# A routed feed-forward kernel: the second product's three terms added up in one PSUM bank

## The chip, the cores and the metric

The kernel runs on one core of a Trainium2 chip. The metric is the device time of one execution in microseconds; lower is better. A core has a matrix engine (TensorE; PE in the profile, its weight loads PEld), a vector engine (VectorE, DVE), a scalar engine (ScalarE, ACT), GpSimd (POOL) and a queue that issues transfers (SyncE, SP). TensorE writes into PSUM, an accumulator memory of eight banks of 512 float32 values per partition; VectorE and ScalarE read it out ("evict" it) into SBUF.

## What is computed

The reference does two things in float32. First a causal convolution of 7 taps along the sequence, with taps that are a softmax over the head's weights. Then a routed feed-forward network: each row picks one of 8 experts, goes through that expert's two matrices with a ReLU between them, and is scaled by the softmax probability of its expert.

```python
B, S, D = 8, 3584, 192; E, F = 8, 1024; N = B * S       # N = 28672 rows
out = np.einsum('hk,bskhg->bshg', w, x_unf)             # w: softmax of weight over 7 taps
...
logits = x @ w_gate + modality_bias[modality_id]
e_idx = np.argmax(logits, axis=1)
gate_w = probs[np.arange(N), e_idx]
for e in range(E):
    mask = e_idx == e
    h = np.maximum(x[mask] @ w1[e], 0.0)
    out[mask] = gate_w[mask, None] * (h @ w2[e])
```

## The kernel before, in words

The convolved rows are computed in groups (lines 222 to 392: products with a band matrix, then the gate's logits, the choice of expert, each row's place), and POOL scatters them to a buffer in DRAM, `routed_rows`, sorted by expert. Beside each row stand its gate and its place in the output. A slot is 512 such rows (256 in the last chunk) of one expert; a pass is 256 rows. `Slot` (from line 602 on) brings a slot's weights and rows, splits the weights, and turns the rows with TensorE transposes.

All large products are done in a format (F32R) in which TensorE takes one pass. To keep accuracy, each factor is split into a high and a low part: `split` casts the high part on ScalarE (L99) and subtracts on VectorE for the low part (L100). A product of two split factors is then three products: high by high, high by low and low by high.

The first product (`first`, L686) makes 256 hidden values for 256 rows: ten products of 256 columns into a bank `hps`, of which ScalarE makes `hh`, the high part of the ReLU (L689), and VectorE `hl`, the low part (L690). The second product (`second`) takes `hh` and `hl` as the stationary operand, 128 hidden values by 128 rows, and streams the second matrix past them. In SBUF that matrix lies as `w2b`: for each block c of 128 hidden values, 192 columns of the high part followed by 192 of the low part. For each block (two in a step) and each half j of the rows, there is one product of `hh` with all 384 columns (L704), which puts high by high into the accumulator's columns 0 to 191 and high by low into 192 to 383, and one of `hl` with the 192 high columns (L708), added to columns 0 to 191. A pass is four steps, eight blocks. Each half has an accumulator `po` of its own, in a bank of its own; there are two such banks (`ps_g2`), so a pass takes both.

After a pass, `put` evicts: for each half ScalarE multiplies the columns 192 to 383 by the gate into `lowp` (L720), VectorE multiplies the columns 0 to 191 by the gate and adds `lowp` (L722) into `o`, one of five buffers, and POOL scatters `o` to the output's rows (L723).

`run` (L810) sets the order: in each step the first product of the step, then the second product of the step two before (LAG = 2), then pieces of the routing work of later rows, as many as are due, splits of the next slot's weights, and at one step of each pass the transposes of the next pass. ScalarE keeps the order in which the program is written (`ORDERED`, L878); the order of the other engines is set by a scheduler.

Of the kernel before, what the change touches and what calls it, by code (L numbers as in the profile page):

```python
# [9 lines left out]
F32 = mybir.dt.float32  # L10
# [3 lines left out]
AF = mybir.ActivationFunctionType  # L14
ALU = mybir.AluOpType
# [3 lines left out]
P = 128  # L19
# [24 lines left out]
def conv_then_routed_ffn(ctx, tc, x, weight, modality, w_gate, mod_bias, w1, w2, out):  # L44
    nc = tc.nc
    NB, S, D = x.shape
    H, K = weight.shape
    E, _, FF = w1.shape
# [6 lines left out]
    NF = FF // P  # L55
    NJ = T // P
# [17 lines left out]
    sp = ctx.enter_context(tc.tile_pool(name="sp", bufs=4))  # L74
    hp = ctx.enter_context(tc.tile_pool(name="hp", bufs=4))
    ps_g1 = ctx.enter_context(tc.tile_pool(name="ps_g1", bufs=2, space=PSUM))
    ps_g2 = ctx.enter_context(tc.tile_pool(name="ps_g2", bufs=2, space=PSUM))
# [5 lines left out]
    def ring(pool, n, shape, dtype, name, tag=None):  # L83

        tag = tag or name
        k = turns[tag] = turns.get(tag, -1) + 1
        return pool.tile(shape, dtype, name=name, tag=f"{tag}_{k % n}", bufs=1)
# [22 lines left out]
    def warm(n):  # L110
# [9 lines left out]
        out=tri, in_=ones, compare_op=ALU.is_gt, fill=0.0, base=0,  # L120
# [481 lines left out]
    class Slot:  # L602
# [90 lines left out]
        def second(self, k, fp):  # L693
            wb = w2b[self.i % 2]
            hh, hl = self.h.pop((k, fp))
            if fp == 0:
                self.po = [ring(ps_g2, 2, [P, 2 * D], F32, "po") for _ in range(NJ)]
            for u in range(2):
                c = 2 * fp + u
                for j, po in enumerate(self.po):  # L700
                    js = slice(j * P, (j + 1) * P)

                    def by_hi():
                        nc.tensor.matmul(po, hh[:, u, js], wb[:, c, :], start=c == 0, stop=c == NF - 1,  # L704
                                         skip_group_check=True)

                    def by_lo():
                        nc.tensor.matmul(po[:, 0:D], hl[:, u, js], wb[:, c, 0:D], start=False, stop=False,  # L708
                                         skip_group_check=True)

                    for product in (by_lo, by_hi) if c == NF - 1 else (by_hi, by_lo):
                        product()
            if fp == NF // 2 - 1:
                self.put(self.h.pop(("tag", k)))

        def put(self, tag):
            for j, po in enumerate(self.po):
                gate = tag[:, j, 0:1]
                lowp = ring(sp, 2, [P, D], F32, "lowp")
                nc.scalar.activation(out=lowp, in_=po[:, D:2 * D], func=AF.Copy, scale=gate)  # L720
                o = ring(sp, OUTS, [P, D], F32, "o")
                nc.vector.scalar_tensor_tensor(out=o, in0=po[:, 0:D], scalar=gate, in1=lowp, op0=ALU.mult, op1=ALU.add)  # L722
                st = nc.gpsimd.indirect_dma_start(  # L723
                    out=out, out_offset=bass.IndirectOffsetOnAxis(ap=tag.bitcast(I32)[:, j, 1:2], axis=0),
                    in_=o, in_offset=None, bounds_check=N - 1, oob_is_err=False).ins
                tc.declare_no_dep(st, group="out", reason="each row is written once")
                tc.add_to_no_dep_group("out", st)
# [3 lines left out]
    for chunk, groups in enumerate(GROUPS_OF_CHUNK):  # L731
# [3 lines left out]
        if chunk == len(GROUPS_OF_CHUNK) - 1:  # L735
            n = (tokens + E * (size - 1)) // size
        else:
            n = SLOTS_OF_CHUNK[chunk]
# [171 lines left out]
```

## Time and profile before

| what | value |
|---|---|
| runs shown | 1309.37 and 1307.13 us, median 1308.25 |
| profiled execution | 1306.6 us |
| its span, first to last instruction | 1304.9 us |
| mean granted TensorE clock | 0.983 |
| POOL busy | 525.4 us (40%) |
| DMA | 140.41 MB, mean 108 GB/s |
| chain that ended last | TensorE 80%, VectorE 6%, POOL 3% |

The profile is of one execution. A row of a group reads: line, engine, operation, tile written <- tiles read, shape and type, count | busy us, mean ns of one | idle time of the engine just before, and what released it. A row of the table by stretch has, for each engine, its busy us and its count of instructions. A row of the timeline has the start and the length in us. Products overlap on TensorE, and the ends of their records are modelled.

### The profile page before, as it was taken

The numbers are of one execution on the slowest core, as the hardware profiler recorded it, in microseconds if no ns is written. First come the engines' busy times: TensorE is split into PE (matmuls) and PEld (weight loads), VectorE is DVE, ScalarE is ACT, GpSimd is POOL, SyncE is SP. The second block draws the span as 40 slices with busy tenths as digits, with TensorE's granted clock in tenths as the row PEclk, the third lists the DMA queues.
The fourth block names the chain that finished last, engine by engine and source line by source line (L and its number), as shares of the span: only waits on it lengthen the run. The fifth ranks groups of instructions, "written<-read, shape, count | busy, mean of one in ns | idle before, by whom it ended". The sixth has DMA issues, their size and how long they took to land.

```text
span 1304.9 us, 27875 instructions
## 1 busy us (share of the span) xinstructions
PE 1253.3 (96%) x9448; PEld 1222.3 (94%) x9448; DVE 1074.7 (82%) x2576; ACT 785.0 (60%) x1828; POOL 525.4 (40%) x574
## 2 busy tenths in 40 slices
PE   8549999999999999999999999999999999999997
PEld 7338899999999999999999999999999999999996
DVE  6459978798889888898889988898888878777895
ACT  2126566566666566766666566666665556555674
POOL 4636753442626244362624435262532612112121
PEclk9859999999999999999999999999999999999999
DMA  5467432352326241453215432352223525353440
GB/s 164 148 172 208 130 117 59 92 151 81 86 65 166 80 116 51 122 157 94 75 45 161 114 96 76 92 158 83 60 61 91 146 67 109 80 156 114 129 117 18
DMA packets 155356, 140.41 MB, mean 108 GB/s; under 512 B 43714, under 2 KB 141627, under 8 KB 155204
## 3 DMA queue, kind: packets, MB, share of 16 engines
q1 hardware_dynamic: 130164, 93.58, 27.3%
q0 software_dynamic: 23232, 44.30, 10.7%
q8 instruction: 76, 1.25, 0.4%
q10 hardware_dynamic: 1808, 0.66, 0.2%
q14 instruction: 76, 0.62, 0.2%
HBM read 160.37 MB, written 48.25 MB: 160 GB/s over the span
## 4 chain that ended last, share of the span: by engine, by line
PE 80%; issue 7%; DVE 6%; POOL 3%; DMA 2%; ACT 1%; POOLq 0%; DVEq 0%; ACTq 0%
PE hps L686 35%; PE po L704 23%; PE po L708 11%; PE cv L274 5%; PE gt L318 3%; POOL routed_rows L211 2%; PE tp L660 1%; DMA routed_rows<-y,idx 1%; POOL out_dram L723 1%; DVE hl L690 1%; PE hps L114 1%; PE tp L661 1%; DMA out_dram<-o,tag 1%; DVE turned L298 1%; DVE gx L100 1%
## 5 line engine op out<-in xcount | busy, mean ns | idle before, releaser
L704 PE MATMUL po<-w2b,hh 128*128 128x384 f32 x1824 | 555.5, 355 | 2.1 <-DVE o L722 1.7
L686 PE MATMUL hps<-sxh,w1b 128*128 128x256 f32 x1824 | 491.7, 292 | 0.5 <-ACT sxh L668 0.4
L689 ACT ACTIVATE hh<-hps 128x512 fp32r<-128x512 f32 x456 | 273.6, 600 | 349.0 <-PE hps L686 342.6
L723 POOL DMA_INDIRECT out_dram<-o,tag x228 | 237.2, 1040 | 530.4 <-DVE o L722 464.6
L708 PE MATMUL po<-w2b,hl 128*128 128x192 f32 x1824 | 440.6, 252 | 0.0
L690 DVE SCALAR_TENSOR_TENSOR hl<-hps,hh 128x512 fp32r<-128x512 f32 x456 | 312.8, 686 | 108.7 <-ACT hh L689 103.6
L686 PE MATMUL hps<-sxs,w1b 128*128 128x256 f32 x1824 | 362.7, 280 | 0.2 <-DVE sxs L670 0.2
L704 PEld LDWEIGHTS po<-w2b,hh 128*128 128x128 f32 x1824 | 343.6, 188 | 5.5 <-DVE o L722 4.8
L686 PEld LDWEIGHTS hps<-sxh,w1b 128*128 128x128 f32 x1824 | 345.0, 189 | 3.7 <-ACT sxh L668 0.6
L708 PEld LDWEIGHTS po<-w2b,hl 128*128 128x128 f32 x1824 | 345.2, 190 | 0.0
L211 POOL DMA_INDIRECT routed_rows<-y,idx x256 | 255.0, 996 | 143.8 <-issue 72.1
L686 PEld LDWEIGHTS hps<-sxs,w1b 128*128 128x128 f32 x1824 | 280.2, 189 | 0.4 <-issue 0.4
L686 PE MATMUL hps<-sxl,w1b 128*128 128x256 f32 x912 | 256.5, 281 | 3.1 <-DVE sxl L670 3.1
L100 DVE TENSOR_TENSOR w1b<-raw,w1b 128x512 fp32r<-128x512 f32 x244 | 164.9, 682 | 19.6 <-ACT w1b L99 17.3
L686 PEld LDWEIGHTS hps<-sxl,w1b 128*128 128x128 f32 x912 | 173.6, 190 | 5.6 <-DVE sxl L670 3.3
L99 ACT CAST w1b<-raw 128x512 fp32r<-128x512 f32 x244 | 149.0, 619 | 0.0
L100 DVE TENSOR_TENSOR w2b<-raw,w2b 128x384 fp32r<-128x384 f32 x244 | 133.0, 551 | 10.2 <-ACT w2b L99 10.0
L99 ACT CAST w2b<-raw 128x384 fp32r<-128x384 f32 x244 | 122.7, 511 | 0.0
L279 ACT COPY y<-cv 112x192 f32<-112x192 f32 (+1 forms) x198 | 53.7, 318 | 96.2 <-PE cv L274 72.3
L720 ACT ACTIVATE lowp<-po,tag 128x192 f32<-128x192 f32 x228 | 83.6, 418 | 31.2 <-PE po L704 31.2
L722 DVE SCALAR_TENSOR_TENSOR o<-po,tag,lowp 128x192 f32<-128x192 f32 x228 | 84.8, 411 | 5.4 <-ACT lowp L720 2.3
L274 PE MATMUL cv<-x,band 128*112 128x384 f32 (+2 forms) x160 | 47.7, 427 | 22.1 <-ACT y L279 19.6
(135 smaller groups left out, 1107.4 us busy)
## 6 DMA issues: line engine op xcount, KB each, us to landing
raw<-in_moe_w_dram SPq DMA_DIRECT2D x61, 768.0 KB
raw<-in_moe_w_dram SPq DMA_DIRECT2D x61, 512.0 KB
raw<-in_moe_w_dram SPq DMA_DIRECT2D x122, 256.0 KB
xr<-in_x_dram SPq DMA_DIRECT2D x36, 384.0 KB
rows<-routed_rows SPq DMA_DIRECT2D x53, 260.0 KB
x<-in_x_dram SPq DMA_DIRECT2D x26, 384.0 KB
ends<-routed_rows SPq DMA_DIRECT2D x53, 128.0 KB
routed_rows<-y,idx POOLq DMA_INDIRECT x256, 2.9
```

The lines of the kernel that those rows point to most:

```text
L99: nc.scalar.copy(out=hi, in_=raw)
L100: return nc.vector.tensor_tensor(out=lo, in0=raw, in1=f(hi), op=ALU.subtract).ins
L211: routed(chunk, nc.gpsimd.indirect_dma_start(out=scr, out_offset=bass.IndirectOffsetOnAxis(ap=idx, axis=0), in_=src, in_offset=None,).ins)
L274: nc.tensor.matmul(cv, wt[:, h, :], xt[:, :, hs], start=n == 0, stop=n == len(terms) - 1)
L686: nc.tensor.matmul(hps[:, u, :], wa[:, c, fs], mv[z], start=n == 0, stop=n == len(terms) - 1)
L689: nc.scalar.activation(out=hh, in_=hps, func=AF.Relu)
L690: nc.vector.scalar_tensor_tensor(out=hl, in0=hps, scalar=0.0, in1=f(hh), op0=ALU.max, op1=ALU.subtract)
L704: nc.tensor.matmul(po, hh[:, u, js], wb[:, c, :], start=c == 0, stop=c == NF - 1, skip_group_check=True)
L708: nc.tensor.matmul(po[:, 0:D], hl[:, u, js], wb[:, c, 0:D], start=False, stop=False, skip_group_check=True)
L720: nc.scalar.activation(out=lowp, in_=po[:, D:2 * D], func=AF.Copy, scale=gate)
L722: nc.vector.scalar_tensor_tensor(out=o, in0=po[:, 0:D], scalar=gate, in1=lowp, op0=ALU.mult, op1=ALU.add)
L723: st = nc.gpsimd.indirect_dma_start(out=out, out_offset=bass.IndirectOffsetOnAxis(ap=tag.bitcast(I32)[:, j, 1:2], axis=0), in_=o, in_offse ...
```

## The change

The accumulator of a pass becomes one tile of 2 x 192 columns in one bank: half j has columns 192 j to 192 j + 191, and all three terms are added up there. The product of `hh` with 384 columns is split into one with the 192 high columns and one with the 192 low columns of `w2b`. In the last block the order of the three terms is reversed. Only the first product into the bank carries the start flag. Two banks are used in turn, one a pass. The eviction is one ScalarE instruction for each half, which multiplies by the gate and writes `o`; `lowp` and VectorE's part are gone.

```diff
@@ second @@
             if fp == 0:
-                self.po = [ring(ps_g2, 2, [P, 2 * D], F32, "po") for _ in range(NJ)]
+                self.po = ring(ps_g2, 2, [P, NJ, D], F32, "po")
             for u in range(2):
                 c = 2 * fp + u
-                for j, po in enumerate(self.po):
+                for j in range(NJ):
                     js = slice(j * P, (j + 1) * P)
-
-                    def by_hi():
-                        nc.tensor.matmul(po, hh[:, u, js], wb[:, c, :], start=c == 0, stop=c == NF - 1,
+                    terms = (hh, 0), (hh, 1), (hl, 0)
+                    if c == NF - 1:
+                        terms = terms[::-1]
+                    for n, (z, w) in enumerate(terms):
+                        nc.tensor.matmul(self.po[:, j, :], z[:, u, js], wb[:, c, w * D:(w + 1) * D],
+                                         start=c == j == n == 0, stop=c == NF - 1 and n == len(terms) - 1,
                                          skip_group_check=True)
-
-                    def by_lo():
-                        nc.tensor.matmul(po[:, 0:D], hl[:, u, js], wb[:, c, 0:D], start=False, stop=False,
-                                         skip_group_check=True)
-
-                    for product in (by_lo, by_hi) if c == NF - 1 else (by_hi, by_lo):
-                        product()
@@ put @@
-            for j, po in enumerate(self.po):
-                gate = tag[:, j, 0:1]
-                lowp = ring(sp, 2, [P, D], F32, "lowp")
-                nc.scalar.activation(out=lowp, in_=po[:, D:2 * D], func=AF.Copy, scale=gate)
+            for j in range(NJ):
                 o = ring(sp, OUTS, [P, D], F32, "o")
-                nc.vector.scalar_tensor_tensor(out=o, in0=po[:, 0:D], scalar=gate, in1=lowp, op0=ALU.mult, op1=ALU.add)
+                nc.scalar.activation(out=o, in_=self.po[:, j, :], func=AF.Copy, scale=tag[:, j, 0:1])
```

On TensorE, in one step in the middle of the program, the order was this from the end of the first product on (output <- streamed operand, stationary operand; the weight loads of these products are part of them and have no row):

```order
L686 MATMUL hps<-sxs,w1b_89 128x256 x2
L704 MATMUL po<-w2b_91,hh 128x384
L708 MATMUL po<-w2b_91,hl 128x192
L704 MATMUL po<-w2b_91,hh 128x384
L708 MATMUL po<-w2b_91,hl 128x192
L704 MATMUL po<-w2b_91,hh 128x384
L708 MATMUL po<-w2b_91,hl 128x192
L704 MATMUL po<-w2b_91,hh 128x384
L708 MATMUL po<-w2b_91,hl 128x192
L274 MATMUL cv<-xh,band_hi 112x384
```

At the same place it now is:

```order
L686 MATMUL hps<-sxs,w1b_89 128x256 x2
L706 MATMUL po<-w2b_91,hh 128x192 x2
L706 MATMUL po<-w2b_91,hl 128x192
L706 MATMUL po<-w2b_91,hh 128x192 x2
L706 MATMUL po<-w2b_91,hl 128x192
L706 MATMUL po<-w2b_91,hh 128x192 x2
L706 MATMUL po<-w2b_91,hl 128x192
L706 MATMUL po<-w2b_91,hh 128x192 x2
L706 MATMUL po<-w2b_91,hl 128x192
L274 MATMUL cv<-xh,band_hi 112x384
```

Eight products became twelve, and what stands before and after them on TensorE is the same.

On ScalarE, at the end of a pass, the order before, with what each instruction waits for (PE for TensorE's products, DMAHW for loads, DMASW for POOL's scatters):

```order
L689 ACTIVATE hh<-hps 128x512 [waits DVE_49,PE_49]
L720 ACTIVATE lowp<-po,tag 128x192 [waits PE_49] x2
L99 CAST xh<-xr 128x768 [waits DMAHW1_49]
L99 CAST w2b_760<-raw_1_88 128x2x192
L668 CAST sxh<-tp 128x256 [waits PE_49]
```

and at such a place now:

```order
L689 ACTIVATE hh<-hps 128x512 [waits DVE_49,PE_49]
L715 ACTIVATE o<-po,tag 128x192 [waits DMASW3_49,PE_49]
L715 ACTIVATE o<-po,tag 128x192 [waits DMASW4_49]
L99 CAST w2b_760<-raw_1_88 128x2x192
L668 CAST sxh<-tp 128x256 [waits PE_49]
```

The two evictions stand where they stood, and each now waits for a scatter too, the one that read its `o` buffer last.

## The prediction

> **What bounds the kernel now.** I read the page's busy shares first, then the table of engines by stretch, then the groups by line and shape, and last the timeline of TensorE's weight loads over one step.
>
> ```profile
> span 1304.9 us, 27875 instructions
> PE 1253.3 (96%) x9448; PEld 1222.3 (94%) x9448; DVE 1074.7 (82%) x2576; ACT 785.0 (60%) x1828; POOL 525.4 (40%) x574
> ```
>
> ```profile
> core 0: us, PE busy (x) PEld busy (x) DVE busy (x) ACT busy (x) POOL busy (x), PEclk, DMA share, GB/s
> 0.00:100.00 100.00, 64.31 (x329) 48.84 (x330) 56.68 (x235) 26.60 (x81) 48.90 (x77) 0.81 0.56 165
> 100.00:200.00 100.00, 95.45 (x685) 88.58 (x684) 88.48 (x220) 60.06 (x143) 66.65 (x69) 1.00 0.49 144
> 200.00:400.00 200.00, 199.73 (x1528) 196.34 (x1527) 172.78 (x405) 127.63 (x295) 78.00 (x83) 1.00 0.34 92
> 400.00:800.00 400.00, 399.12 (x3068) 395.82 (x3066) 351.52 (x810) 259.19 (x599) 177.94 (x192) 1.00 0.38 105
> 800.00:1200.00 400.00, 399.53 (x3110) 397.92 (x3109) 326.23 (x751) 245.06 (x563) 131.99 (x133) 1.00 0.37 99
> 1200.00:1295.00 95.00, 95.00 (x741) 94.79 (x740) 78.30 (x159) 65.83 (x150) 19.96 (x20) 1.00 0.35 100
> ```
>
> The columns that matter are PE and PEld, TensorE's products and its weight loads. From 200 us to 1295 us PE is idle for 0.27 + 0.88 + 0.47 + 0 = 1.6 us of 1095, at a granted clock of 1.00. Nothing else can set the time there: VectorE's 82% and ScalarE's 60% lie beside a TensorE that never waits. So each nanosecond added to TensorE's sequence goes onto the end one for one, and work taken off VectorE buys nothing. But PE busy is made of overlapping products (a record lasts until its result is out), so the price of a product is the distance between starts, not its recorded length. The groups show why that matters:
>
> ```profile
> L704 PE MATMUL po<-w2b,hh 128*128 128x384 f32 x1824 | 555.5, 355 | 2.1 <-DVE o L722 1.7
> L708 PE MATMUL po<-w2b,hl 128*128 128x192 f32 x1824 | 440.6, 252 | 0.0
> L704 PEld LDWEIGHTS po<-w2b,hh 128*128 128x128 f32 x1824 | 343.6, 188 | 5.5 <-DVE o L722 4.8
> L708 PEld LDWEIGHTS po<-w2b,hl 128*128 128x128 f32 x1824 | 345.2, 190 | 0.0
> ```
>
> The second product is 1824 pairs: one product of 384 columns, one of 192, each with a weight load of its own. Four pairs make a step, so there are 1824 / 4 = 456 steps. If recorded lengths were prices, a pair would take 355 + 252 = 607 ns, and 1824 of them 1107 us, 85% of the span with the first product still to be placed. They overlap, so the starts are what to read. Here is one step of the second product, TensorE's loads and three of its products (start, length):
>
> ```profile
> 1231.93 0.19 PEld L708 LDWEIGHTS po<-w2b,hl 128*128 128x128 f32 x1
> 1232.11 0.19 PEld L704 LDWEIGHTS po<-w2b,hh 128*128 128x128 f32 x1
> 1232.21 0.19 PEld L708 LDWEIGHTS po<-w2b,hl 128*128 128x128 f32 x1
> 1232.39 0.19 PEld L704 LDWEIGHTS po<-w2b,hh 128*128 128x128 f32 x1
> 1232.50 0.19 PEld L708 LDWEIGHTS po<-w2b,hl 128*128 128x128 f32 x1
> 1232.68 0.19 PEld L704 LDWEIGHTS po<-w2b,hh 128*128 128x128 f32 x1
> 1232.79 0.19 PEld L708 LDWEIGHTS po<-w2b,hl 128*128 128x128 f32 x1
> 1232.96 0.19 PEld L686 LDWEIGHTS hps<-sxh,w1b 128*128 128x128 f32 x1
> 1233.07 0.19 PEld L686 LDWEIGHTS hps<-sxl,w1b 128*128 128x128 f32 x1
> ```
>
> ```profile
> 1231.93 0.34 PE L704 MATMUL po<-w2b,hh 128*128 128x384 f32 x1
> 1232.10 0.25 PE L708 MATMUL po<-w2b,hl 128*128 128x192 f32 x1
> 1232.19 0.36 PE L704 MATMUL po<-w2b,hh 128*128 128x384 f32 x1
> ```
>
> The load for the next product starts when the present product starts to stream, and runs beside it. From 1231.93 to 1233.07 is 1.14 us for four pairs, 0.285 a pair. The distances alternate. After a load for hl (that is, while the 384 columns stream) they are 0.18, 0.18, 0.18, 0.17, mean 0.178. After a load for hh, or the last one for w1b (while the 192 columns stream), they are 0.10, 0.11, 0.11, 0.11, mean 0.108. The first 384-column product passes on after 0.17, so 192 columns are worth 0.085 to 0.09 of streaming, and the product rows say the same (1232.10 to 1232.19). The next load nevertheless starts only after 0.108: what is late is the load, not the columns. **A load of 128 columns cannot follow the one before it by less than about 0.108 us**; 384 columns hide that, 192 do not. The transposes, of only 128 columns, show the same floor:
>
> ```profile
> 1230.52 0.14 PEld L661 LDWEIGHTS tp<-ident,ends 128*128 128x128 f32 x1
> 1230.63 0.19 PEld L686 LDWEIGHTS hps<-sxh,w1b 128*128 128x128 f32 x1
> 1230.74 0.19 PEld L686 LDWEIGHTS hps<-sxl,w1b 128*128 128x128 f32 x1
> ```
>
> That is 0.11 twice. The mean of the six distances is (0.43 + 0.22) / 6 = 0.1083 us, the floor that I use.
>
> **The change part by part.** *Products.* Each pair (384, 192) becomes three products of 192: the same 576 columns, but three loads where there were two, 1824 more products and loads in all. Now a pair costs 0.285: one product bound by its columns, one by its load. In the change all three are bound by the load: 3 x 0.1083 = 0.325. A step goes from 1.14 to 12 x 0.1083 = 1.30 us, and 456 steps times 0.16 are **+73 us**. The step's two ends stay as they are, since the last product of a step is one of 192 before and after. Bounds from the rows: from below, if every product were bound by its columns alone (0.0875), a step would be 1.05 us, -0.09 x 456 = -41 us. From above, the distance that the first product's loads keep, beside 256 columns:
>
> ```profile
> 1233.07 0.19 PEld L686 LDWEIGHTS hps<-sxl,w1b 128*128 128x128 f32 x1
> 1233.19 0.19 PEld L686 LDWEIGHTS hps<-sxh,w1b 128*128 128x128 f32 x1
> ```
>
> 0.12, or 12 x 0.12 = 1.44 us a step, +0.30 x 456 = +137 us. I take 0.1083, since the rows it comes from stand in this very sequence, beside the same 192 columns.
>
> *The same weights twice.* In each triple hh is loaded for w2's high part and at once again for its low part. Does the second load count? The program has such neighbours already: the gate multiplies each block of wg_parts with gx's high and low part in turn.
>
> ```profile
> L318 PE MATMUL gt<-gx,wg_parts 128*128 128x256 f32 x336 | 49.9, 298 | 11.8 <-ACT gx L99 8.0 <-DVE gx L100 3.6
> L318 PEld LDWEIGHTS gt<-gx,wg_parts 128*128 128x128 f32 x336 | 44.7, 198 | 14.7 <-ACT gx L99 9.5 <-DVE gx L100 4.6 <-DVE y L281 0.3
> L114 PE MATMUL hps<-ones 112*112 112x448 bf16 x50 | 12.3, 404 | 1.2 <-DVE ones L109 1.2
> L114 PEld LDWEIGHTS <-ones 112*112 112x112 bf16 x50 | 7.4, 149 | 5.7 <-issue 1.7 <-DVE ones L109 1.2
> ```
>
> 336 products, 336 loads, though every second load brings what is there; the warm-up loads the same ones 50 times for 50 products. So the repeated load is issued, and I count it in full.
>
> *Evictions.* VectorE loses 228 instructions of 411 ns; ScalarE keeps 228 of the same shape, which now write o.
>
> ```profile
> L722 DVE SCALAR_TENSOR_TENSOR o<-po,tag,lowp 128x192 f32<-128x192 f32 x228 | 84.8, 411 | 5.4 <-ACT lowp L720 2.3 <-DMA out_dram<-o,tag 2.1 <-ACT w2b L99 1.0
> L720 ACT ACTIVATE lowp<-po,tag 128x192 f32<-128x192 f32 x228 | 83.6, 418 | 31.2 <-PE po L704 31.2
> L689 ACT ACTIVATE hh<-hps 128x512 fp32r<-128x512 f32 x456 | 273.6, 600 | 349.0 <-PE hps L686 342.6 <-issue 1.2
> ```
>
> The 84.8 us lie beside TensorE and are worth 0, but for the last eviction after the last product, some 0.4 us. ScalarE takes over the wait for a free o, which the output's scatter on POOL's queue must have read: 2.1 us in all on VectorE now. Behind it on ScalarE stand the casts of the next weights and hh, for which TensorE waits. But ScalarE itself idles 343 us waiting for TensorE ahead of hh, and the second product runs two steps after the first (LAG), about 2 x 2.33 us by the starts of the loads (1230.74 for one step's second load, 1233.07 for the next), so 2.1 us spread over the program cost 0. Without that cover they would cost those 2.1 us.
>
> *The banks.* Each pass's two accumulators shared two banks, so the next pass waited for the eviction: PEld 4.8 us and PE 1.7 us behind o, partly the same waits. With both halves in one bank and two banks in turn, that wait goes: I take **-4 us**, between 0 and -6.5. Nothing is late in its place: a bank is written again a whole pass after its eviction could begin.
>
> **Sum.** The profiled execution took 1306.6 us with its span of 1304.9. 1306.6 + 73 - 4 - 0.4 = 1375 us. The median of the runs shown, 1308.25, lies 1.65 above that execution, so about 1377; the rows are read to 0.01 us and a floor of 0.109 would add 4, so I say **1378 us**, 5.3% above now.
>
> **Rivals.** *Columns alone* (the other side): the load queue runs ahead far enough that 192-column products follow each other at 0.0875. Its place is all 456 steps, its price -41 - 4, the time 1263 us. It decides from a load distance below 0.095 (a third of 0.285); the rows above, 0.10 to 0.11 four times out of four beside just such products, speak against it. The Trainium skill, "TensorE: Matmul & The Clock Gate", section "Back-to-back issue gap", has a rule of this kind: a sustained stream of loads and products takes about 81 ns a product at 128 columns and 131 ns at 512. A line between these gives an estimate of 89 ns at 192, 12 x 0.089 = 1.07 us a step, about -32 us and 1272. The trace here disagrees (0.11 where only 128 columns stream), and the same page's section "LDWEIGHTS (loading the stationary operand)", columns / 1.2 or 107 ns, agrees with it.
>
> *The repeated load is free.* Then hh streams 2 x 0.0875, hl's load hides behind that, and the triple costs 0.175 + 0.108 = 0.283: the pair's price. 1308 - 4 = 1304 us, no change. The 336 loads for 336 products speak against it; the trace can't show whether such a load is shorter, because 256 columns cover it.
>
> *Loads at the wider distance*, 0.12 instead of 0.1083, because they now follow without a break: +137 - 4, 1441 us. Against it: the transposes' loads follow each other at 0.11 with no long stream among them.
>
> *ScalarE becomes the bound* through its new wait: every one of 114 evictions would have to outlast two steps before TensorE noticed. Its share is 60%, and the wait is 2.1 us in all; between 0 and +2 us, inside the range.
>
> **How the numbers follow.** A measurement of this kernel can tell about 2% from no change, 26 us. My forecast has 0.86: all triples bound by the load, 1362 to 1396 (a floor of 0.1055 to 0.112 us in the same sum: 12 x 0.1055 = 1.27 and 12 x 0.112 = 1.34 us a step). The wider distance and other additions beyond 1396 get 0.08, all slower. The free repeated load gets 0.04 (same), columns alone 0.02 (faster). So faster 0.02, same 0.04, slower 0.94. The range 1362 to 1396 leaves out 0.14.
>
> **What would show it.** In the changed profile: L706 with 5472 products and 5472 loads; loads of the second product 0.108 apart without alternation; a step of that product 1.30 us long; PE still idle for next to nothing after 200 us; VectorE at some 990 us busy and no PE wait for an eviction. Loads 0.09 apart, or two loads for three products, would make the forecast wrong; so would PE idle time of tens of microseconds behind ScalarE.

## The result and the profile after

The changed kernel takes 1391.21 us (median of 1390.91 and 1391.51) where the kernel before takes 1308.25: a ratio of 1.0633, 95% interval 1.0615 to 1.0650. It is 83 us slower; 1378 were forecast, with 1362 to 1396 as the range. The profiled execution took 1390.9 us. Its page begins:

```profile
span 1389.2 us, 31268 instructions
PE 1337.7 (96%) x11272; PEld 1312.5 (94%) x11272; DVE 997.3 (72%) x2348; ACT 780.9 (56%) x1828; POOL 524.2 (38%) x574
```

TensorE has 11272 - 9448 = 1824 more products and as many more loads; VectorE has 228 instructions fewer and 77 us less to do. The table by stretch of the changed kernel (the same columns as in the prediction) shows which of the two counts:

```profile
200.00:400.00 200.00, 200.00 (x1716) 197.59 (x1716) 150.87 (x336) 117.23 (x271) 76.43 (x84) 1.00 0.29 81
400.00:800.00 400.00, 399.85 (x3447) 399.20 (x3446) 309.78 (x710) 242.15 (x561) 158.50 (x170) 1.00 0.36 100
800.00:1200.00 400.00, 400.00 (x3476) 399.55 (x3475) 285.81 (x655) 232.99 (x540) 139.97 (x144) 1.00 0.32 86
1200.00:1380.00 180.00, 180.00 (x1585) 180.00 (x1583) 117.22 (x228) 106.95 (x244) 36.33 (x34) 1.00 0.37 106
```

After 200 us TensorE is idle for 0.15 us in all, at a granted clock of 1.00: it is still the only bound, and it has more to do. The groups of the second product and its eviction, changed kernel:

```profile
L706 PE MATMUL po<-w2b,hh 128*128 128x192 f32 x3648 | 630.4, 272 | 0.0
L706 PEld LDWEIGHTS po<-w2b,hh 128*128 128x128 f32 x3648 | 555.7, 191 | 0.0
L706 PE MATMUL po<-w2b,hl 128*128 128x192 f32 x1824 | 481.2, 274 | 0.0
L706 PEld LDWEIGHTS po<-w2b,hl 128*128 128x128 f32 x1824 | 341.3, 192 | 0.0
L715 ACT ACTIVATE o<-po,tag 128x192 f32<-128x192 f32 x228 | 83.6, 417 | 88.1 <-PE po L706 84.9 <-DMA out_dram<-o,tag 3.1
```

There are 5472 products and 5472 loads, so the second load of hh is there each time. The idle column is 0.0 where the kernel before had 1.7 and 4.8 us behind an eviction. And this is one step of the second product, the weight loads in order of time (x2 joins two neighbours; the second of a row of 0.30 starts 0.30 - 0.19 = 0.11 after the first):

```profile
1280.58 0.31 PEld L706 LDWEIGHTS po<-w2b,hh 128*128 128x128 f32 x2
1280.81 0.19 PEld L706 LDWEIGHTS po<-w2b,hl 128*128 128x128 f32 x1
1280.92 0.30 PEld L706 LDWEIGHTS po<-w2b,hh 128*128 128x128 f32 x2
1281.14 0.19 PEld L706 LDWEIGHTS po<-w2b,hl 128*128 128x128 f32 x1
1281.26 0.30 PEld L706 LDWEIGHTS po<-w2b,hh 128*128 128x128 f32 x2
1281.48 0.19 PEld L706 LDWEIGHTS po<-w2b,hl 128*128 128x128 f32 x1
1281.59 0.30 PEld L706 LDWEIGHTS po<-w2b,hh 128*128 128x128 f32 x2
1281.81 0.19 PEld L706 LDWEIGHTS po<-w2b,hl 128*128 128x128 f32 x1
1281.92 0.19 PEld L686 LDWEIGHTS hps<-sxh,w1b 128*128 128x128 f32 x1
```

The alternation of 0.18 and 0.11 is gone. Twelve loads take 1281.92 - 1280.58 = 1.34 us, 0.112 each, against 1.14 us for eight. 456 steps times 0.20 are 91 us. Read over all steps after 200 us, the median from a step's first load to the first load behind the step is 1.148 us before and 1.343 now, and 456 times 0.195 are 89 us. The span grew by 84.3. The waits for evictions that are gone make up for part of the products (before, 1.7 us on TensorE and 4.8 on its loads, partly the same). Against them stands a stretch of lower clock: behind two waits of TensorE for the gate's rows, 1.27 and 1.37 us, the granted clock is 0.50 from 160 to 165 us and products stand 0.21 us apart, where the kernel before has 1.00; I estimate some 3 us from these rows. So the balance closes to a few microseconds, not better.

### The profile page after: what moved, and what is told of

It reads as the page before. It is cut to its first block, busy times and chain, and to the rows that moved or that the text cites. A ratio compares the mean times of both kernels' runs of the same rounds, so it can differ in the third digit from the quotient of the medians.

```text
span 1389.2 us, 31268 instructions
## 1 busy us (share of the span) xinstructions
PE 1337.7 (96%) x11272; PEld 1312.5 (94%) x11272; DVE 997.3 (72%) x2348; ACT 780.9 (56%) x1828; POOL 524.2 (38%) x574
## 4 chain that ended last, share of the span: by engine, by line
PE 66%; issue 1%; POOL 0%; DMA 0%; ACT 0%; DVE 0%; POOLq 0%; ACTq 0%
PE po L706 32%; PE hps L686 29%; PE cv L274 2%; PE gt L318 2%; PE tp L660 1%; PE tp L661 1%; DMA out_dram<-o,tag 0%; POOL out_dram L716 0%; POOL routed_rows L211 0%; ACT hh L689 0%; ACT gx L99 0%; ACT w2b L99 0%; DVE hl L690 0%; PE rp L367 0%; PE rp L368 0%
## 5 line engine op out<-in xcount | busy, mean ns | idle before, releaser
L706 PE MATMUL po<-w2b,hh 128*128 128x192 f32 x3648 | 630.4, 272 | 0.0
L706 PEld LDWEIGHTS po<-w2b,hh 128*128 128x128 f32 x3648 | 555.7, 191 | 0.0
L686 PE MATMUL hps<-sxh,w1b 128*128 128x256 f32 x1824 | 491.5, 292 | 0.5 <-ACT sxh L668 0.4
L706 PE MATMUL po<-w2b,hl 128*128 128x192 f32 x1824 | 481.2, 274 | 0.0
L686 PE MATMUL hps<-sxs,w1b 128*128 128x256 f32 x1824 | 363.2, 281 | 0.3 <-DVE sxs L670 0.3
L686 PEld LDWEIGHTS hps<-sxh,w1b 128*128 128x128 f32 x1824 | 346.2, 190 | 3.6 <-ACT sxh L668 0.6
L706 PEld LDWEIGHTS po<-w2b,hl 128*128 128x128 f32 x1824 | 341.3, 192 | 0.0
L686 PEld LDWEIGHTS hps<-sxs,w1b 128*128 128x128 f32 x1824 | 280.5, 190 | 0.4 <-issue 0.4
L686 PE MATMUL hps<-sxl,w1b 128*128 128x256 f32 x912 | 256.7, 281 | 3.3 <-DVE sxl L670 3.3
L686 PEld LDWEIGHTS hps<-sxl,w1b 128*128 128x128 f32 x912 | 174.0, 191 | 5.7 <-DVE sxl L670 3.5
L715 ACT ACTIVATE o<-po,tag 128x192 f32<-128x192 f32 x228 | 83.6, 417 | 88.1 <-PE po L706 84.9
L100 DVE TENSOR_TENSOR gx<-turned,gx 128x768 fp32r<-128x768 f32 x56 | 53.5, 955 | 23.8 <-ACT gx L99 23.3
```

What stands on the lines that cost most here:

```text
L100: return nc.vector.tensor_tensor(out=lo, in0=raw, in1=f(hi), op=ALU.subtract).ins
L686: nc.tensor.matmul(hps[:, u, :], wa[:, c, fs], mv[z], start=n == 0, stop=n == len(terms) - 1)
L706: nc.tensor.matmul(self.po[:, j, :], z[:, u, js], wb[:, c, w * D:(w + 1) * D], start=c == j == n == 0, stop=c == NF - 1 and n == len(terms ...
L715: nc.scalar.activation(out=o, in_=self.po[:, j, :], func=AF.Copy, scale=tag[:, j, 0:1])
```

## The experiments

**Theory:** a load of 128 weight columns can follow the one before it only after 0.11 us, so a product costs the longer of that and its own streaming (0.0875 us for 192 columns). **Rivals:** the columns set the distance; each load and product has a fixed cost of issue; a repeated load of the same weights is special; part of the loss comes from the single bank or from ScalarE's eviction.

The first four runs fell on a chip where every kernel ran 200 to 250 us longer, before too (1542.7 us there). In the trace of the eviction alone from that chip, ScalarE stands idle ahead of `hh` for 177.7 us in 19 waits whose releaser the profile doesn't show, and TensorE for 35 to 49 us ahead of the products of each of L686, L704 and L708 with nothing shown to wait for. That the engines waited for their instructions, as the expectations say, fits this but is not shown. These times are given but not built upon; the same kernels were run again on other chips.

### The products alone

```diff
 def by_hi():
-    nc.tensor.matmul(po, hh[:, u, js], wb[:, c, :], start=c == 0, ...)
+    for w in range(2):
+        nc.tensor.matmul(po[:, w * D:(w + 1) * D], hh[:, u, js], wb[:, c, w * D:(w + 1) * D], start=c == w == 0, ...)
```

> The three products of 192 columns, but with the two banks of a pass and both evictions as before. Theory (the load sets each product's distance): the whole loss is here. The changed profile shows loads 0.111 to 0.112 us apart, a step of 1.34 us against 1.14, so 1308 + 456 x 0.20 = 1399 us, up to 8 less where waits of before go into the longer step: 1391 to 1400. Rival (part of the loss comes from the single bank or from the eviction on the scalar engine): clearly under 1391, by that part.

Measured there: 1601.9 us, a ratio of 1.0376 (1.0346 to 1.0407), which decides nothing, since TensorE's products alone do not set the time there.

> The kernel of products_alone once more, because there all kernels, before too, ran some 230 us longer, with ScalarE and TensorE waiting now and then for their instructions. Where they don't: theory, as there, before + 83 to 92 us (1391 to 1400 where before takes 1308), TensorE idle below 1% after 200 us. Rival (the single bank or the eviction cost part of the loss): clearly under before + 83.

Measured: 1397.95 us, 1.0680 (1.0658 to 1.0702), +89 us. The whole loss is in the products, as the theory has it. The changed kernel's 1.0633 lies 0.0047 below, 6 us: bank and eviction do not cost, they give. The groups of this run still have the wait for VectorE's eviction, and more of it than the kernel before (1.7 and 4.8 us there), so a few of the 89 us are this wait and not the loads:

```profile
L705 PE MATMUL po<-w2b,hh 128*128 128x192 f32 x3648 | 632.0, 272 | 5.6 <-DVE o L723 5.6
L705 PEld LDWEIGHTS po<-w2b,hh 128*128 128x128 f32 x3648 | 555.5, 191 | 7.7 <-DVE o L723 7.1
```

### The eviction alone

```diff
-lowp = ring(sp, 2, [P, D], F32, "lowp")
-nc.scalar.activation(out=lowp, in_=po[:, D:2 * D], func=AF.Copy, scale=gate)
-nc.vector.scalar_tensor_tensor(out=o, in0=po[:, 0:D], scalar=gate, in1=lowp, op0=ALU.mult, op1=ALU.add)
+nc.scalar.activation(out=o, in_=po[:, 0:D], func=AF.Copy, scale=gate)
```

> The products of before, 384 and 192 columns in two banks; the eviction is the scalar engine's alone and reads columns 0 to 191. The high by low term is computed and left out of the output. Theory: nothing hangs on the vector engine's part, 1302 to 1309 us. Rival (the scalar engine's new wait for a free output buffer delays hh): over 1312 us.

Measured: 1524.7 us, 0.988 (0.9855 to 0.9905) of before's 1542.7; again with those idle stretches.

> The kernel of evict_alone once more, where engines do not wait for instructions. The high by low term is computed and left out of the output. The changed kernel took 6 to 7 us less than the products alone, so bank and eviction together gave that. Theory (the bank gave it, the eviction nothing): 1306 to 1310 us where before takes 1308. Rival (the eviction without the vector engine gave it): 1300 to 1304.

Measured: 1303.5 us, 0.9957 (0.9941 to 0.9973), 5 us less. Here my expectation fell: the rival had 1300 to 1304. The group of the loads for hh in this run says how:

```profile
L704 PEld LDWEIGHTS po<-w2b,hh 128*128 128x128 f32 x1824 | 343.9, 189 | 0.7 <-ACT o L720 0.6
```

4.8 us of waiting for an eviction became 0.6, though the banks are as before. An eviction of one ScalarE instruction frees the bank sooner than one that goes on to VectorE; whether the second instruction or VectorE's queue made the difference is not kept apart here. So the spare bank and the shorter eviction remove the same wait, and either alone is enough for most of it.

### Fewer columns, the same loads

```diff
-nc.tensor.matmul(self.po[:, j, :], z[:, u, js], wb[:, c, w * D:(w + 1) * D], ...)
+wide = D if c == n == 0 else 128
+nc.tensor.matmul(self.po[:, j, 0:wide], z[:, u, js], wb[:, c, w * D:w * D + wide], ...)
```

> As the changed kernel, but the products of the second stage stream 128 columns instead of 192 (only the first product of each accumulator keeps 192); the sums of the last 64 columns are left out. Theory (load sets the distance): the same time as the changed kernel, 1383 to 1392 us, loads still 0.108 to 0.112 us apart. Rival (the columns set it): 0.111 x 128 / 192 = 0.074 us a product, 456 x 12 x 0.037 = 203 us less, about 1188 us.

Measured: 1636.6 us, 1.0609 (1.0573 to 1.0646) of before's time there.

> The kernel of cols128 once more, for its time. Theory (the load sets the distance): as the changed kernel, before + 80 to 84. Rival (the columns set it): before - 120.

Measured: 1386.4 us, 1.0592 (1.0573 to 1.0611), +78 us, 2 us less than the theory's lower end and 198 more than the rival's. A third of the second product's streaming is gone and next to nothing is gained (5 us against the changed kernel). Ten loads in a row of this run, the first and the last:

```profile
1282.22 0.31 PEld L707 LDWEIGHTS po<-w2b,hh 128*128 128x128 f32 x2
...
1283.34 0.30 PEld L707 LDWEIGHTS po<-w2b,hh 128*128 128x128 f32 x2
```

1.12 us for ten: still 0.112 each.

### More columns, the same loads

The accumulator is [P, NJ, 256] in both; the low part's columns are taken from further left, so that they stay inside the block.

```diff
-nc.tensor.matmul(self.po[:, j, :], z[:, u, js], wb[:, c, w * D:(w + 1) * D], ...)
+nc.tensor.matmul(self.po[:, j, 0:224], z[:, u, js], wb[:, c, w * (2 * D - 224):w * (2 * D - 224) + 224], ...)
```

> As the changed kernel, but each product of the second stage streams 224 columns; the last 32 sums of each are not used, and the low part's columns are taken from 32 further left, so its term is another one. Theory: 224 columns take 224 / 2.18 = 0.103 us, still less than a load of 0.111, so the time of the changed kernel, before + 83. Rival (the columns set it): 0.111 x 224 / 192 = 0.130, another 102 us, before + 185.

Measured: 1390.3 us, 1.0627 (1.0601 to 1.0653): the changed kernel's time, with 17% more columns.

> As cols224, with 256 columns. Theory: 256 columns take 0.1175 us as in the first product, now more than the load: 12 x 0.1175 = 1.41 against 1.34 us a step, another 33 us, before + 116. Rival (the columns set it at the rate of the changed kernel's 192 in 0.111): another 203 us, before + 286.

Measured: 1418.4 us, 1.0834 (1.0815 to 1.0853), +110 us, 27 more than the changed kernel. From the first load of a step to the first load of the first product after it, with 224 columns and then with 256:

```profile
1282.22 0.30 PEld L706 LDWEIGHTS po<-w2b,hh 128*128 128x128 f32 x2
...
1283.56 0.19 PEld L686 LDWEIGHTS hps<-sxh,w1b 128*128 128x128 f32 x1
```

```profile
1283.19 0.30 PEld L706 LDWEIGHTS po<-w2b,hh 128*128 128x128 f32 x2
...
1284.59 0.19 PEld L686 LDWEIGHTS hps<-sxh,w1b 128*128 128x128 f32 x1
```

1.34 us with 224, as with 192; 1.40 with 256, and 456 times 0.06 are the 27 us. From 128 to 224 columns a product costs the same; between 224 and 256 the columns begin to count.

### Smaller loads, the same columns

```diff
-nc.tensor.matmul(self.po[:, j, :], z[:, u, js], wb[:, c, w * D:(w + 1) * D], ...)
+high = P if c == n == 0 else 64
+js = slice(j * P, j * P + high)
+nc.tensor.matmul(self.po[0:high, j, :], z[:, u, js], wb[:, c, w * D:(w + 1) * D], ...)
```

> As the changed kernel, but the second stage loads 64 weight columns (64 of each 128 rows) instead of 128 and streams 192 columns as there; half the rows' sums are left out. Theory (the load sets the distance, and its length goes with the weight columns): a load of some 0.055 us hides behind 192 columns, 0.0875 us a product, 12 x 0.0875 = 1.05 against 1.34 us a step, 132 us less, about 1259 us. Rival (a fixed cost of issuing a load and a product, whatever their size): 1391 us, no change against the changed kernel.

Measured: 1529.7 us, 0.992 (0.9894 to 0.9946) of before's 1542.7.

> The kernel of rows64 once more, for its time without those waits. Its loads stood 0.087 to 0.092 us apart, 0.090 in the middle. By the theory a step of the second product is then 12 x 0.090 = 1.08 us against 1.14 before: 456 x 0.06 = 27 us less, and 4 to 7 for waits, so before - 31 (about 1277 us where before takes 1308), 114 less than the changed kernel. Rival (fixed cost of issue): as the changed kernel, before + 83.

Measured: 1308.6 us, 0.9995 (0.9982 to 1.0008). Against the changed kernel that is 83 us less, which a fixed cost of issue excludes: it issues the same number of loads and products. The loads, the end of a step:

```profile
1281.92 0.13 PEld L708 LDWEIGHTS po<-w2b,hh 128*64 128x64 f32 x1
1282.01 0.13 PEld L708 LDWEIGHTS po<-w2b,hl 128*64 128x64 f32 x1
1282.10 0.23 PEld L708 LDWEIGHTS po<-w2b,hh 128*64 128x64 f32 x2
1282.28 0.13 PEld L708 LDWEIGHTS po<-w2b,hl 128*64 128x64 f32 x1
1282.37 0.19 PEld L686 LDWEIGHTS hps<-sxh,w1b 128*128 128x128 f32 x1
1282.48 0.19 PEld L686 LDWEIGHTS hps<-sxl,w1b 128*128 128x128 f32 x1
```

They stand 0.09 apart, the time of 192 columns, until the first load of 128 columns, which takes 0.11 again. But I had expected before - 31, so 31 us are missing. Part is that each step holds one distance set by 128 weight columns, 0.11 - 0.09 = 0.02, 9 us; read over all steps after 200 us the median step is 1.115 us against 1.148 before, so 15 us less where I had 27. For the rest there are new waits; the longest, from this run's timeline (start, length, idle before and what ended it):

```profile
1032.26 0.42 ACT L717 ACTIVATE o<-po,tag 128x192 f32<-128x192 f32 x1 [3.46 <-DMA out_dram<-o,tag]
1033.91 0.60 ACT L689 ACTIVATE hh<-hps 128x512 fp32r<-128x512 f32 x1
1035.18 0.69 DVE L690 SCALAR_TENSOR_TENSOR hl<-hps,hh 128x512 fp32r<-128x512 f32 x1
1035.92 0.58 PE L686 MATMUL hps<-sxh,w1b 128*128 128x256 f32 x1 [2.74 <-DVE hl L690]
```

ScalarE waits 3.46 us for a free o, hh behind it comes late, hl after that, and TensorE, which needs the bank that both read, stands still for 2.74 us. Behind it the granted clock is 0.64 from 1036 to 1040 us, and the next loads of 128 columns stand 0.21 apart. In this run TensorE waits 8.2 us for hl (its loads 12.9), where it waited 0.2 (loads 0.4) in the changed kernel. This is the mechanism of the prediction's last rival, at a small price: ScalarE's wait for o reaches TensorE. That it does so because TensorE is 6% faster than in the changed kernel is not shown: the eviction alone ran as fast (1303.5 us) with an eviction on ScalarE too, and there ScalarE's waits for o were at most 1.13 us, against 2.5 to 4.1 here, and TensorE's loads waited 0.3 us for hl. Why the waits for o are longer here is open. The longer step (12 us) and the waits for hl (8 to 13) are 20 to 25 of the 31 us, the lower clock one or two more by estimate; what the remaining part is, I did not settle.

### No weights twice in a row

```diff
-terms = (hh, 0), (hh, 1), (hl, 0)
+terms = (hh, 0), (hl, 0), (hh, 1)
```

> The changed kernel with the product of hl between the two of hh, so that no weights are loaded twice in a row. Theory (every load counts alike): the changed kernel's time, before + 81 to 85, loads 0.111 to 0.112 us apart. Rival (loading the same weights again is what costs more than the floor of 0.108 seen before): loads 0.108 apart, 12 x 0.0035 x 456 = 19 us less, before + 64.

Measured: 1392.1 us, 1.0634 (1.0614 to 1.0654): the changed kernel's ratio. Five loads of this run:

```profile
1282.10 0.19 PEld L706 LDWEIGHTS po<-w2b,hl 128*128 128x128 f32 x1
1282.21 0.30 PEld L706 LDWEIGHTS po<-w2b,hh 128*128 128x128 f32 x2
1282.43 0.19 PEld L706 LDWEIGHTS po<-w2b,hl 128*128 128x128 f32 x1
1282.54 0.19 PEld L706 LDWEIGHTS po<-w2b,hh 128*128 128x128 f32 x1
1282.65 0.19 PEld L686 LDWEIGHTS hps<-sxh,w1b 128*128 128x128 f32 x1
```

0.55 us for five. A load costs the same whether or not its weights are already there.

### A third bank, with the products of before

```diff
-return ring(ps_t, 4, *args, "t")
+return ring(ps_t, 3, *args, "t")
...
-self.po = [ring(ps_g2, 2, [P, 2 * D], F32, "po") for _ in range(NJ)]
+self.po = [ring(ps_g2, 3, [P, 2 * D], F32, "po") for _ in range(NJ)]
```

The other uses of the two rings, at the start of the program among them, have the same numbers.

> The kernel before, with three banks in turn for the second product's accumulators and three instead of four for the convolution and the transposes. It tells what the changed kernel's free bank is worth by itself, and is meant as a version that is faster than both. Theory: TensorE's waits for an eviction (6.5 us in the trace of before, partly the same twice) go, 1302 to 1308 us where before takes 1308. Rival (the bank taken from the convolution stalls it): over 1310 us.

Measured: 1298.5 us, 0.9933 (0.9912 to 0.9955), 10 us less than before and 93 less than the changed kernel: the fastest version here that computes all terms. The wait of hh's loads for an eviction is mostly gone (4.8 us to 0.9), and so is a wait of the first product; first two groups of the kernel before, where the second shows that wait, then the same two with the third bank:

```profile
L704 PEld LDWEIGHTS po<-w2b,hh 128*128 128x128 f32 x1824 | 343.6, 188 | 5.5 <-DVE o L722 4.8
L686 PE MATMUL hps<-sxl,w1b 128*128 128x256 f32 x912 | 256.5, 281 | 3.1 <-DVE sxl L670 3.1
```

```profile
L704 PEld LDWEIGHTS po<-w2b,hh 128*128 128x128 f32 x1824 | 343.7, 188 | 1.5 <-DVE o L722 0.9
L686 PE MATMUL hps<-sxl,w1b 128*128 128x256 f32 x912 | 256.2, 281 | 0.0
```

The first is what the bank was meant to do. The second, 3.1 us, is one wait at the first slot, which I had not counted on; that the order of the start differs with the third bank is the likely reason, but it was not tested. The start is the larger part: the profiled span is 7.8 us shorter, and 4.7 us of that are there when the third step's first product begins, 109 us into the program. So this run does not price the wait for evictions by itself; what came after the start is 3 us.

## Why the prediction was right, and where it was off

**The bound.** TensorE was the only bound after 200 us, and it stayed so. VectorE's 77 us bought nothing; what came of the eviction (5 us by itself) came from a bank that was free sooner.

**The products.** The mechanism held: every product of 128 to 224 columns costs one load. The term was mis-sized: 12 x 0.1083 = 1.30 us a step was forecast, 1.34 came, so 89 to 91 us in place of 73. In the changed kernel the median distances within a step are 0.118 behind the first product's 256 columns, then 0.109 and 0.111, and 0.112 for all that follow. So 0.108 is what a load keeps shortly behind a longer stream, and 0.112 what it keeps in an unbroken row. Four of my six distances were of the first kind; the two at the transposes, which I also held against a wider distance, stand in a row of only four loads behind 384 columns. 0.112 was the upper end of my range (0.1055 to 0.112), so the result lies near its edge; the 0.12 that I gave 0.08 did not come. Nor is the floor one for every pair of loads, as I had put it: in the changed kernel the second load of the transposes starts 0.069 us behind the first (median), whose own start is late, while the products there keep 0.11. The order of the terms does not matter for it (the run with hl between), nor the columns (128, 192 and 224).

**The repeated load** counts in full, as argued from the gate's 336 loads: 5472 loads, and the same time with hl between.

**The banks.** -4 us was taken, between 0 and -6.5; the products alone against the changed kernel give 6 us, though the products alone wait longer for evictions than the kernel before did. That the shorter eviction frees the old banks too was missing from the prediction, which gave the eviction nothing but the last 0.4 us.

**ScalarE's new wait** costs next to nothing here, as forecast: 3.1 us on ScalarE in two waits, 0.2 on TensorE. But the cover is smaller than the 2 x 2.33 us that I took for it: the longer of the two waits is 1.98 us, and hl is late for TensorE 4.5 us behind it, by 0.15 us. In the run with smaller loads, waits of 2.5 to 4.1 us cost TensorE 0.8 to 2.7 us each.

**The sum.** By the medians over all steps the products came out 16 us dearer (18 by the rows shown), and the lower clock near 160 us cost some 3 us by estimate; some 2 us more of waits went than I took, and about 1 had been added in rounding up. That makes 16, where 13 lie between 1378 and 1391; I can't place the 3 us between.

## What to carry to other kernels

Where TensorE never waits, as here, count each product as the longer of its streaming and its weight load, from the distances between starts and not from the records' lengths: splitting one product of 384 columns into two of 192 adds a whole load, though the columns stay the same. Before work is moved away from an engine for the sake of its busy share, look whether the engine that sets the end ever waits for it; a wait of a few microseconds for a bank may be removed more cheaply by one more bank (here one that the convolution could spare).

## What the runs showed of the hardware

Loads of 128 weight columns stand 0.108 us apart where a longer stream lies between the loads before, and 0.112 where each follows the last without a break; with 64 weight columns 0.09, where 192 columns set it. Products of 128, 192 and 224 columns took the same 0.112, products of 256 columns 0.117. What makes 0.112 out of 0.108 is open. The second load of weights that are already there is neither skipped nor shorter. After TensorE had stood idle for 2.74 us, its granted clock fell to 0.64 over the next four microseconds, and loads of 128 columns stood 0.21 us apart.
